# Pooled attention feeding two expert layers: pooled keys that carry the softmax scale, first scores in two halves, first values summed on TensorE

## The chip, the cores and the metric

The kernel runs as one program on one core of a Trainium2 chip. The metric is the device time of one execution in microseconds (us). A core has five engines that run side by side and meet at semaphores: TensorE (PE; its weight loads are listed as PEld), VectorE (DVE), ScalarE (ACT), GpSimd (POOL) and SyncE (SP), which issues nearly all of the transfers (DMA) between memory and the core. Each engine works through its own instructions strictly in the order in which the program lists them.

## The reference

Attention with pooled keys and values, then a layer of four gated experts, then a normalised gated layer. Only the first stage is touched:

```python
k_p = k.reshape(B, H, Sp, pool, D).mean(axis=3)      # B=4, H=8, S=576, D=64, pool=8, Sp=72
v_p = v.reshape(B, H, Sp, pool, D).mean(axis=3)
scores = scale * np.matmul(q, k_p.transpose(0, 1, 3, 2))   # scale = 1/sqrt(D)
scores = scores - np.max(scores, axis=-1, keepdims=True)
attn = np.exp(scores)
attn = attn / (np.sum(attn, axis=-1, keepdims=True) + 1e-09)
attn_out = np.matmul(attn, v_p)
# x = attn_out as 2304 tokens x 512
# then  out = sum_e p_e * relu(x @ w1[e]) @ w2[e],  E=4, F=1024
# then  (silu(xn @ w_gate) * (xn @ w_val)) @ w_out  with xn the rms-normalised out
```

## The kernel before

**Tiles.** The 2304 tokens are 18 tiles of 128. The expert layers run in three passes of six tiles. Tiles 0 to 5 are attended before and between the first expert products, tiles 6 to 17 beside them. A batch has 576 tokens, so tiles 0 to 3 use keys and values of batch 0 alone, tile 4 uses batches 0 and 1, and tile 5 batch 1.

**One tile of attention**, as steps with their names in the order table (i is the tile): `sc` is the scores (8 TensorE passes: four products of the queries of a pair of heads with the pooled keys `kpb`, each float32 product being two passes); `mx` is the row maximum and its multiplication by -SCALE (L1087, L1088, VectorE); `ex` is eight exponentials, one per head, with the scale and the maximum as operands and the row sum as a second output (L1094, ScalarE); `nm` normalises (L1106 to L1108, VectorE); `tr` is eight transposes (L1120, TensorE); `ca` and `cd` copy their two halves out of PSUM (ScalarE, VectorE); `av` is the product with the pooled values `vpb` (L1154, TensorE); `rw` copies it out (L1171, ScalarE); `ha`, `hd`, `l0`, `l1` cut it into a rounded part and a rest for the expert products.

**Pooling.** `Lk0a`, `Lk0b` load the keys of batch 0 (two pairs of heads each), `k0a`, `k0b` add the eight tokens of a pool (L1009, VectorE) and put the sums into `kpb` (L1016, ScalarE). `Lv0a` to `Lv0d` load the values of batch 0, two heads each. `v0a`, `v0b`, `v0c` add them on TensorE, by eight accumulating products with an identity matrix (L1042), and `vc` copies the sums out (L1049); `v0d` adds on GpSimd (L991, L1045). The values of batch 1 (`v1a` to `v1d`) are all added on GpSimd, its keys on VectorE with a copy into `kpb` by GpSimd (L1014). `Lv0d` and `Lv1c` use one buffer, `vr`: the second load waits until the first has been read.

**Order.** The text `ORDER` (L55 to L63) lists the steps up to the fourth expert block, and every engine gets its instructions in this order. `heatN` are N products of the identity with itself on TensorE, which nothing reads. `p000`, `p001` and so on are the first expert products (`by_half`, L558 to L560), which need tiles 0 to 2; `sc4`, the scores of tile 4, needs the pooled keys of batch 1. `ws0` prepares the first weights on GpSimd (L321 to L325), `wh0` rounds them on VectorE (L307), `t00`, `t10` on ScalarE (L331).

**Transfers.** SP issues in the order of the table and stops at the first one that may not go. Each transfer reports on one of eight semaphores in turn, so it waits, beside its buffer, for the landing of the one eight before it. The queries of tiles 0 and 1 go through ScalarE's queue.

Of the kernel before, what the change touches and what calls it, by code (L numbers as in the profile page):

```python
# [11 lines left out]
F32 = mybir.dt.float32  # L12
# [14 lines left out]
P = 128  # L27
NPAIR = H // 2
# [5 lines left out]
TT = NST // NPASS  # L34
# [17 lines left out]


ORDER = """
Lq0 heat24 Lk0a Lq1 k0a ow0 Lk0b k0b Lv0a or0 sc0 Lw0 Lv0b ws0 v0a xo mx0 ex0 Lv0d sc1 t00 v0d Lq2 wh0 Lv0c  # L55
mx1 ex1 v0b nm0 sc2 Lq3 mx2 ex2 nm1 tr0 cd0 nm2 Lx1 v0c ca0 tr1 ow2 Lv1c cd1 Lv1a vc av0 ca1 rw0 tr2 wl0 hd0
ha0 Lq4 av1 ca2 cd2 av2 l10 rw1 swap Lk1a sc3 Lk1b Lq5 hd1 ha1 l00 rw2 Lv1b v1b l11 ha2 Lx0 xh01 hd2 free0 l01
t10 l02 ow1 Lw1 l12 p000 heat12 mx3 k1a p001 xl01 ex3 r000 or1 s000 xh00 nm3 tr3 v1a wh1 k1b ca3 Ld cd3 av3
# [9 lines left out]
def tile_kernel(ctx: ExitStack, tc, qp, kp, vp, dp, w1r, w2r, w64, rg, out):  # L68
    nc = tc.nc
# [53 lines left out]
    xo = [{}, {}]  # L123
# [865 lines left out]
    def halve(cut):  # L989
        for w in (4, 2):  # L990
            nc.gpsimd.tensor_tensor(cut(0, w), cut(0, w), cut(w, 2 * w), op=ALU.add)  # L991

    def spare(tag):
        return late["sb"].tile([P, 4 * N], F32, name="stg", tag=tag, bufs=4 if tag == "hA" else 3)

    def pool_k(b, j, stage=None, eng=None):

        if stage is None:
            stage = at["sb"].tile([P, 2 * S], F32, name="kr", tag="kr")
        else:  # L1000
            stage = spare(stage)
        stage = stage[:, :2 * S].rearrange("p (j s k) -> p j s k", j=2, k=POOL)
        for i in range(2):
            nc.sync.dma_start(stage[:, i], kp[b, j + i].rearrange("p (s k) -> p s k", k=POOL))
        yield
        if eng is nc.vector:
            for i in range(2):
                c = at["sb"].tile([P, SP], F32, name="kc", tag="kc", bufs=2)
                nc.vector.tensor_reduce(c, stage[:, i], axis=AX.X, op=ALU.add)  # L1009
                for hh in range(2):  # L1010
                    sl = slice(64 * hh, 64 * hh + 64)
                    o = kpb[b % 2][sl, j + i, hh, :]
# [12 lines left out]
    def pool_v(b, h, stage=None, eng=None, queue=nc.sync):
# [35 lines left out]
    def att_a(i):  # L1061
        att_sc(i)
        att_ex(i)

    SCALE = 1.0 / (POOL * math.sqrt(D))

    def att_sc(i):
        q = q_t.pop(i)
        if at["few"]:
            sc = at["ps"].tile([P, 2, 512], F32, name="sc", tag="at")  # L1070
        else:
            sc = at["ps"].tile([P, 2, 512], F32, name="sc", tag="sc", bufs=2)
# [7 lines left out]
        es_t[i] = sc[:, :, 0:4 * SP].rearrange("p a (h s) -> p a h s", h=4)  # L1080

    def att_mx(i):
        v = es_t[i]
        m = at["sb"].tile([P, H], F32, name="m", tag="m", bufs=2)
        sm = at["sb"].tile([P, H], F32, name="sm", tag="sm", bufs=2)
        es = at["sb"].tile([P, H, SP], F32, name="es", tag="es", bufs=2)
# [12 lines left out]
    def att_a(i):
        att_sc(i)  # L1100
        att_mx(i)
        att_ex(i)
# [100 lines left out]
    def run(queue, k=1, one=False):  # L1203
# [165 lines left out]
    for si, ((moe, p), ids) in enumerate(stages):  # L1369
# [3 lines left out]
        for i in ids[2 * (si == 0):]:  # L1373
            k, _, e, r = quads[i]
# [132 lines left out]
```

## Time and profile before

| | |
|---|---|
| time, median of 3 runs | 1265.5 us (1264.29 to 1267.74) |
| profiled execution, span from first to last instruction | 1264.4 us |
| TensorE busy | 1242.1 us, 98% of the span |
| VectorE, ScalarE, GpSimd busy | 833.4, 529.3, 264.6 us |
| first expert product | at 27.27 us |

The span is that of one execution under the profiler; the runs were timed without it. The span ends with the last instruction, and no separate time of the profiled execution is listed, so the median stands beside it: it is 1.1 us more. A busy engine need not be the one that the others wait for, and a share of the span is a mean over stages that differ: the first 40 us are attention and loading, the rest is dominated by products of 384 and 512 columns.

### The profile page before, as it was taken

The page shows a single profiled execution, that of the slowest core. Times are in us where ns is not written, and L with a number is a line of the kernel's source. Part 1 is how long each engine was busy: PE and PEld are TensorE (multiplying, and loading weights), DVE is VectorE, ACT ScalarE, POOL GpSimd, SP SyncE. Part 2 cuts the span into 40 slices and gives each one's busy share as a digit, 9 for nine tenths or more (in the row PEclk, how much of TensorE's full clock was granted, in tenths as well). Part 3 has the DMA queues.
Part 4 walks back from the last instruction along what each step waited for, and adds up shares of the span by engine and source line. Part 5 has one row for each costly group of instructions (what it writes and reads, how often), then busy time and mean ns, then how long its engine had stood idle before and what let it go on. Part 6 is the DMA issues. An engine that isn't in the chain of part 4 may idle for free.

```text
span 1264.4 us, 18367 instructions
## 1 busy us (share of the span) xinstructions
PE 1242.1 (98%) x6876; PEld 1149.0 (91%) x6876; DVE 833.4 (66%) x1335; ACT 529.3 (42%) x1211; POOL 264.6 (21%) x252
## 2 busy tenths in 40 slices
PE   8999999999999999999999999999999999999998
PEld 8889888988898888888889998888999999999998
DVE  6866656656557766644877776475567765786575
ACT  6564544444453333323443343255454434434331
POOL 3434433420112222200333332131220000000000
PEclk9999999999999999999999999999999999999999
DMA  8488687778787777665889988667777777867671
GB/s 262 164 314 300 241 288 252 278 288 303 262 304 266 264 285 268 230 236 198 311 300 346 317 322 304 248 229 278 301 289 272 256 292 263 307 249 298 225 268 51
DMA packets 118937, 339.15 MB, mean 268 GB/s; under 512 B 10304, under 2 KB 48192, under 8 KB 99648
## 3 DMA queue, kind: packets, MB, share of 16 engines
q1 hardware_dynamic: 118560, 337.46, 73.7%
q8 instruction: 54, 0.88, 0.3%
q10 hardware_dynamic: 288, 0.52, 0.1%
q14 instruction: 35, 0.29, 0.1%
HBM read 233.61 MB, written 104.33 MB: 267 GB/s over the span
## 4 chain that ended last, share of the span: by engine, by line
PE 83%; DVE 8%; DMA 4%; ACT 3%; issue 1%; POOL 0%; SPq 0%; ACTq 0%; DVEq 0%; POOLq 0%
PE py L876 9%; PE py L875 9%; PE py L874 9%; PE qX L523 8%; PE qX L525 8%; PE qX L524 8%; PE qY L523 4%; PE qY L525 4%; PE qY L524 4%; PE qZ L523 2%; PE qZ L525 2%; PE qZ L524 2%; DMA wt<-wt_d 1%; PE gy L821 1%; DMA wc_d<-cx 1%; PE gy L823 1%
## 5 line engine op out<-in xcount | busy, mean ns | idle before, releaser
L892 DVE SCALAR_TENSOR_TENSOR y<-py,dps,y 128x512 f32<-128x512 f32 x126 | 94.4, 750 | 180.9 <-PE py L876 180.8
L438 POOL TENSOR_TENSOR cx<-cx 128x512 f32<-128x512 f32 x36 | 50.2, 1394 | 381.7 <-ACT hB L578 84.9
L523 PE MATMUL qX<-xos,wt 128*128 128x384 f32 x328 | 113.6, 346 | 6.5 <-ACT s L531 4.5
L876 PE MATMUL py<-w,hB 128*128 128x512 f32 x288 | 113.6, 395 | 0.0
L875 PE MATMUL py<-w,hB 128*128 128x512 f32 x288 | 113.4, 394 | 0.0
L876 PE MATMUL py<-w,hA 128*128 128x512 f32 x288 | 113.4, 394 | 0.0
L875 PE MATMUL py<-w,hA 128*128 128x512 f32 x288 | 113.4, 394 | 0.0
L874 PE MATMUL py<-w,hA 128*128 128x512 f32 x288 | 112.4, 390 | 0.0
L874 PE MATMUL py<-w,hB 128*128 128x512 f32 x288 | 112.1, 389 | 0.0
L525 PE MATMUL qX<-xos,wt 128*128 128x384 f32 x328 | 111.2, 339 | 0.0
L524 PE MATMUL qX<-xos,wt 128*128 128x384 f32 x328 | 110.8, 338 | 0.0
L578 ACT ACTIVATE hB<-u 128x768 fp32r<-128x768 f32 x46 | 39.1, 849 | 141.3 <-DVE u L535 138.7
L528 ACT ACTIVATE qZ<-qX 128x384 f32<-128x384 f32 x81 | 38.9, 480 | 118.2 <-PE qX L525 83.1
L533 DVE TENSOR_TENSOR u<-qY,s 128x384 f32<-128x384 f32 x82 | 45.5, 554 | 64.6 <-PE qY L525 34.1
L531 ACT ACTIVATE s<-qX 128x384 f32<-128x384 f32 x83 | 40.7, 490 | 108.5 <-PE qX L525 108.5
L263 POOL TENSOR_TENSOR tw<-rw 128x512 f32<-128x512 f32 x25 | 36.8, 1474 | 222.4 <-DVE wt L281 168.9
L523 PEld LDWEIGHTS qX<-xos,wt 128*128 128x128 f32 x328 | 61.9, 189 | 14.3 <-ACT s L531 6.2
L876 PEld LDWEIGHTS py<-w,hB 128*128 128x128 f32 x288 | 54.0, 188 | 11.6 <-DVE hB L564 0.2
L524 PEld LDWEIGHTS qX<-xos,wt 128*128 128x128 f32 x328 | 61.9, 189 | 2.7
L876 PEld LDWEIGHTS py<-w,hA 128*128 128x128 f32 x288 | 54.0, 188 | 11.4
L874 PEld LDWEIGHTS py<-w,hA 128*128 128x128 f32 x288 | 54.2, 188 | 10.1 <-issue 0.2
L875 PEld LDWEIGHTS py<-w,hA 128*128 128x128 f32 x288 | 54.0, 188 | 10.2 <-DVE w L378 0.3
(224 smaller groups left out, 3514.4 us busy)
## 6 DMA issues: line engine op xcount, KB each, us to landing
wt<-wt_d SPq DMA_DIRECT2D x56, 1024.0 KB
w<-w_d SPq DMA_DIRECT2D x32, 1024.0 KB
wt_d<-wt SPq DMA_DIRECT2D x28, 1024.0 KB
wr<-wr_d SPq DMA_DIRECT2D x56, 512.0 KB
wr_d<-wr SPq DMA_DIRECT2D x28, 768.0 KB
cr<-w SPq DMA_DIRECT2D x36, 512.0 KB
w<-ws_d SPq DMA_DIRECT2D x18, 1024.0 KB
w_d<-w SPq DMA_DIRECT2D x16, 1024.0 KB
```

The costliest lines, as they stand in the source:

```text
L438: nc.gpsimd.tensor_tensor(x, x, m.bitcast(F32), op=ALU.mult)
L523: nc.tensor.matmul(bank[b], wh, xh, start=first and k == 0, stop=False, **kw)
L524: nc.tensor.matmul(bank[b], wh, xl, start=False, stop=False, **kw)
L525: nc.tensor.matmul(bank[b], wl, xh, start=False, stop=k == 1, **kw)
L528: nc.scalar.activation(v, bank[b], AF.Copy)
L531: nc.scalar.activation(s[n], bank[b], AF.Copy)
L533: nc.vector.tensor_tensor(u[:, 0], bank["Y"], s[2], op=ALU.add)
L578: nc.scalar.activation(h[:, 0], u, AF.Relu)
L874: nc.tensor.matmul(ps, lhs[0], w[:, 0, c], start=j == 0, stop=False)
L875: nc.tensor.matmul(ps, lhs[0], w[:, 1, c], start=False, stop=False)
L876: nc.tensor.matmul(ps, lhs[1], w[:, 0, c], start=False, stop=j == len(units) - 1)
L892: nc.vector.scalar_tensor_tensor(y_t[t], ps, gate, y_t[t], op0=ALU.mult, op1=ALU.add)
```

## The change

- The pooled keys hold minus SCALE times the sum, so that the row extreme of the raw scores is a minimum, which is the bias of the exponential as it stands; the multiplication of the maximum (L1088) is gone from every tile, and the exponential has scale -1. For batch 0 ScalarE's copy into `kpb` multiplies. For batch 1 GpSimd's copy becomes a multiplication. For batches 2 and 3 GpSimd's last addition goes over all 128 rows and two multiplications follow it.
- The keys of batch 0 are loaded and summed in four steps (`Lk00` to `Lk03`, `k00` to `k03`), pairs 0 and 2 through SP's queue and pairs 1 and 3 through ScalarE's. All queries go through SP's.
- Scores, minimum and exponentials of tile 0 are cut into two halves of four heads (`sc0l`, `mx0l`, `ex0l`, `sc0h`, `mx0h`, `ex0h`).
- `v0d` adds on TensorE, and `vc` copies all eight heads. `cc0`, a copy on VectorE, replaces `ca0` on ScalarE.
- The order table up to `p000` is written anew.

```diff
 ORDER = """
-Lq0 heat24 Lk0a Lq1 k0a ow0 Lk0b k0b Lv0a or0 sc0 Lw0 Lv0b ws0 v0a xo mx0 ex0 Lv0d sc1 t00 v0d Lq2 wh0 Lv0c
...
+Lk00 Lk01 heat18 Lq0 Lk03 Lk02 Lq1 ow0 or0 Lw0 Lq2 k00 k01 sc0l k02 k03 mx0l ex0l heat4 sc0h Lv0a mx0h ex0h xo
...
-                    if b:
-                        nc.gpsimd.tensor_copy(o, c[sl])
-                    else:
-                        nc.scalar.activation(o, c[sl], AF.Copy)
+                    nc.gpsimd.tensor_scalar(o, c[sl], -SCALE, None, op0=ALU.mult)
         else:
             halve(lambda a, b: stage[..., a:b])
+            nc.gpsimd.tensor_tensor(stage[..., 0], stage[..., 0], stage[..., 1], op=ALU.add)
             for hh in range(2):
                 sl = slice(64 * hh, 64 * hh + 64)
-                o = kpb[b % 2][sl, j:j + 2, hh, :]
-                nc.gpsimd.tensor_tensor(o, stage[sl, ..., 0], stage[sl, ..., 1], op=ALU.add)
+                nc.gpsimd.tensor_scalar(kpb[b % 2][sl, j:j + 2, hh, :], stage[sl, ..., 0], -SCALE, None, op0=ALU.mult)
...
+    def first_k(j, queue):
+        if j // 2 not in k_raw:
+            k_raw[j // 2] = spare("hA")[:, :2 * S].rearrange("p (j s k) -> p j s k", j=2, k=POOL)
+        queue.dma_start(k_raw[j // 2][:, j % 2], kp[0, j].rearrange("p (s k) -> p s k", k=POOL))
+
+    def first_k_sum(j):
+        c = at["sb"].tile([P, SP], F32, name="kc", tag="kc", bufs=2)
+        nc.vector.tensor_reduce(c, k_raw[j // 2][:, j % 2], axis=AX.X, op=ALU.add)
+        for hh in range(2):
+            sl = slice(64 * hh, 64 * hh + 64)
+            nc.scalar.activation(kpb[0][sl, j, hh, :], c[sl], AF.Copy, scale=-SCALE)
...
-        for j in range(NPAIR):
+        for j in pairs:
...
-        nc.vector.tensor_reduce(m.rearrange("p (a h) -> p a h", a=2), v, axis=AX.X, op=ALU.max)
-        nc.vector.tensor_scalar(m, m, -SCALE, None, op0=ALU.mult)
...
+        nc.vector.tensor_reduce(
+            m.rearrange("p (a h) -> p a h", a=2)[:, half], v[:, half], axis=AX.X, op=ALU.min
+        )
...
-        for h in range(H):
+        for h in heads:
             nc.scalar.activation(
-                es[:, h], v[:, h // 4, h % 4], AF.Exp, bias=m[:, h:h + 1], scale=SCALE, accum_out=sm[:, h:h + 1]
+                es[:, h], v[:, h // 4, h % 4], AF.Exp, bias=m[:, h:h + 1], scale=-1.0, accum_out=sm[:, h:h + 1]
             )
...
-    def att_cd(i):
+    def att_cd(i, a=1):
         aT, tr = aT_t[i]
-        nc.vector.tensor_copy(aT[:, 4:], tr[1])
-        tr[1] = None
+        nc.vector.tensor_copy(aT[:, 4 * a:4 * a + 4], tr[a])
+        tr[a] = None
...
-        (0, "hA", nc.tensor), (2, "hB", nc.tensor), (4, "hB", nc.tensor), (6, None, None)
+        (0, "hA", nc.tensor), (2, "hB", nc.tensor), (4, "hB", nc.tensor), (6, None, nc.tensor)
...
-        "swap": swap, "xo": first_xo, "gates": gates, "vc": lambda: v_copy(6),
+        "swap": swap, "xo": first_xo, "gates": gates, "vc": lambda: v_copy(8),
...
-        step(f"Lq{i}", load_q, i, nc.scalar if i < 2 else nc.sync)
+        step(f"Lq{i}", load_q, i)
+    for j in range(NPAIR):
+        step(f"Lk0{j}", first_k, j, nc.scalar if j % 2 else nc.sync)
+        step(f"k0{j}", first_k_sum, j)
+    for a, c in enumerate("lh"):
+        step("sc0" + c, att_sc, 0, range(2 * a, 2 * a + 2))
+        step("mx0" + c, att_mx, 0, slice(a, a + 1))
+        step("ex0" + c, att_ex, 0, range(4 * a, 4 * a + 4))
+    for i in range(TT):
+        step(f"cc{i}", att_cd, i, 0)
```

In the orders that follow, `sc<-kpb,y` are scores, `vs` the sums of values of batch 0 (two heads in eight products), `tr` transposes, `av` the products with the values. TensorE before, from the first instruction to the scores of tile 3:

```order
L1059 MATMUL heat<-ident 128x128 x24
L1076 MATMUL sc<-kpb_88,y 128x144 x4
L1042 MATMUL vs<-stg,ident 72x128 x8
L1076 MATMUL sc<-kpb_88,y 128x144 x4
L1042 MATMUL vs<-stg,ident 72x128 x8
L1076 MATMUL sc<-kpb_88,y 128x144 x4
L1120 MATMUL tr<-ident,es 72x128 x8
L1042 MATMUL vs<-stg,ident 72x128 x8
L1120 MATMUL tr<-ident,es 72x128 x8
L1154 MATMUL av<-aT,vpb_90 64x128 x8
L1120 MATMUL tr<-ident,es 72x128 x8
L1154 MATMUL av<-aT,vpb_90 64x128 x16
```

TensorE of the changed kernel in the same place, after its 18 first heat products, the first two score products of tile 0 and four heat products:

```order
L1095 MATMUL sc<-kpb_88,y 128x144 x2
L1070 MATMUL heat<-ident 128x128 x4
L1095 MATMUL sc<-kpb_88,y 128x144 x4
L1070 MATMUL heat<-ident 128x128 x2
L1053 MATMUL vs<-stg,ident 72x128 x8
L1095 MATMUL sc<-kpb_88,y 128x144 x4
L1053 MATMUL vs<-stg,ident 72x128 x8
L1142 MATMUL tr<-ident,es 72x128 x8
L1053 MATMUL vs<-stg,ident 72x128 x8
L1142 MATMUL tr<-ident,es 72x128 x8
L1053 MATMUL vs<-vr,ident 72x128 x8
L1176 MATMUL av<-aT,vpb_90 64x128 x16
```

There are 28 heat products in place of 24, ten of them behind the first scores; a fourth group of value sums, `vs<-vr`, stands behind the transposes of tile 1, and the products of tiles 0 and 1 with the values now stand behind it.

The start of TensorE's order in the changed kernel once more, with the semaphores that an instruction waits for (`DVE_49` and `Activation_49` count VectorE's and ScalarE's instructions, the `DMAHW` ones transfers):

```order
L1070 MATMUL heat<-ident 128x128 x17
L1095 MATMUL sc<-kpb_88,y 128x144 [waits DMAHW1_49,Activation_49,Pool_49]
L1095 MATMUL sc<-kpb_88,y 128x144 [waits Activation_49]
L1070 MATMUL heat<-ident 128x128 x4
L1095 MATMUL sc<-kpb_88,y 128x144 [waits DVE_49,Activation_49]
L1095 MATMUL sc<-kpb_88,y 128x144
L1070 MATMUL heat<-ident 128x128 x4
```

The third score product of tile 0 has a wait on VectorE, at the count of `mx0l`, and one on ScalarE, at the count of the fourth exponential of `ex0l`; before, the four products had waits on ScalarE for the pooled keys alone.

SP's queue before, from the load of `v0d` into `vr` (first row) to the next load into `vr`, that of `v1c`, and what follows it:

```order
L1034 DMA vr<-vp 72x1024 [waits DMAHW1_49]
L986 DMA y<-qp 128x512 [waits DMAHW2_49]
L1034 DMA stg<-vp 72x1024 [waits DMAHW3_49]
L986 DMA y<-qp 128x512 [waits DMAHW4_49]
L352 DMA stg<-w2r 128x1024 [waits DMAHW5_49]
L1034 DMA vr<-vp 72x1024 [waits DMAHW6_49,DMAHW1_49,Pool_49]
L1034 DMA stg<-vp 72x1024 [waits DMAHW7_49]
L986 DMA y<-qp 128x512 [waits DMAHW0_49]
```

The same place of SP's queue in the changed kernel:

```order
L1045 DMA vr<-vp 72x1024 [waits DMAHW3_49]
L986 DMA y<-qp 128x512 [waits DMAHW4_49]
L352 DMA stg<-w2r 128x1024 [waits DMAHW5_49,DVE_49]
L1045 DMA vr<-vp 72x1024 [waits DMAHW6_49,DMAHW3_49,PE_49]
L1045 DMA stg<-vp 72x1024 [waits DMAHW7_49]
L986 DMA y<-qp 128x512 [waits DMAHW0_49]
```

The load of `v1c` waited for GpSimd's sum of `v0d` and now waits for TensorE's; behind it, in both, stand the loads of `v1a`, of tile 4's queries, of the keys of batch 1, of tile 5's queries and of `v1b`.

## Rows read from the trace of the kernel before

**Rows 1.** The page, part 1: busy time of TensorE.

```profile
PE 1242.1 (98%) x6876; PEld 1149.0 (91%) x6876; DVE 833.4 (66%) x1335; ACT 529.3 (42%) x1211; POOL 264.6 (21%) x252
```

**Rows 2.** Windows: stretch, its length, busy time of each engine, clock, DMA.

```profile
9.24:27.27 18.03, 15.67 (x153) 13.96 (x152) 14.95 (x31) 13.52 (x62) 5.77 (x6) 1.00 0.88 267
27.27:38.70 11.43, 10.46 (x90) 9.49 (x89) 8.35 (x15) 7.01 (x25) 8.95 (x15) 1.00 0.32 106
```

**Rows 3.** Timeline of TensorE: start, duration, line, tile; idle time before in brackets.

```profile
1.39 7.85 PE L1059 MATMUL heat<-ident 128*128 128x128 f32 x48 [1.39 <-POOL ident masks.py:199]
...
10.06 1.91 PE L1042 MATMUL vs<-stg,ident 72*72 72x128 f32 x16
11.81 1.15 PE L1076 MATMUL sc<-kpb,y 128*128 128x144 f32 x8
...
21.54 1.09 PE L1154 MATMUL av<-aT,vpb 72*64 72x128 f32 x16
22.56 1.07 PE L1120 MATMUL tr<-ident,es 128*72 128x128 f32 x8
23.56 1.97 PE L1154 MATMUL av<-aT,vpb 72*64 72x128 f32 x32
26.28 1.25 PE L1076 MATMUL sc<-kpb,y 128*128 128x144 f32 x8 [0.76 <-ACT stg L1171]
27.27 0.43 PE L558 MATMUL qX<-xoa,wr 128*128 128x384 f32 x1
...
29.45 2.84 PE L1059 MATMUL heat<-ident 128*128 128x128 f32 x24
```

**Rows 4.** Timeline of TensorE at the scores of tile 4.

```profile
38.04 1.04 PE L1076 MATMUL sc<-kpb,y 128*64 128x144 f32 x6 [0.60 <-POOL kpb L1014]
```

**Rows 5.** Timeline of GpSimd up to 38.6 us.

```profile
16.19 0.85 POOL L1045 TENSOR_TENSOR vpb<-vr 72x128 f32<-72x128 f32 x1
28.96 2.41 POOL L991 TENSOR_TENSOR stg<-stg 72x512 f32<-72x512 f32 x2 [11.93 <-DMA stg<-vp]
31.45 0.45 POOL L1045 TENSOR_TENSOR vpb<-stg 72x128 f32<-72x128 f32 x1
31.85 1.56 POOL L1014 COPY kpb<-kc 64x72 f32<-64x72 f32 x4
33.49 2.08 POOL L991 TENSOR_TENSOR stg<-stg 72x512 f32<-72x512 f32 x2
35.64 1.87 POOL L1045 TENSOR_TENSOR vpb<-stg 72x128 f32<-72x128 f32 x1
37.46 1.11 POOL L1014 COPY kpb<-kc 64x72 f32<-64x72 f32 x4
```

**Rows 6.** Timeline of SP's issues: the loads of v1c and v1b.

```profile
17.06 0.32 SPq L1034 DMA_DIRECT2D vr<-vp  x1
...
20.72 0.35 SPq L1034 DMA_DIRECT2D stg<-vp  x1
```

**Rows 7.** Timeline of VectorE and ScalarE.

```profile
11.05 1.18 DVE L1088 TENSOR_SCALAR m<-m 128x8 f32<-128x8 f32 x1
...
12.33 0.32 ACT L1094 ACTIVATE es<-sc,m 128x72 f32<-128x72 f32 x1 [2.98 <-DVE m L1088]
...
13.53 0.33 ACT L1094 ACTIVATE es<-sc,m 128x72 f32<-128x72 f32 x1
...
23.67 0.69 DVE L1135 COPY aT<-tr 72x512 f32<-72x512 f32 x1
...
25.65 0.58 ACT L1171 ACTIVATE stg<-av 128x512 f32<-128x512 f32 x1
```

**Rows 8.** Windows of TensorE alone: length, busy, clock, DMA.

```profile
84.60:86.80 2.20, 0.14 (x1) 1.00 0.85 137
...
88.00:91.50 3.50, 3.50 (x13) 0.51 1.02 433
91.50:95.00 3.50, 3.50 (x19) 1.00 1.01 387
```

More of the change, by code (lines that the diff above doesn't have):

```diff
@@ L54 @@
 ORDER = """
-Lq0 heat24 Lk0a Lq1 k0a ow0 Lk0b k0b Lv0a or0 sc0 Lw0 Lv0b ws0 v0a xo mx0 ex0 Lv0d sc1 t00 v0d Lq2 wh0 Lv0c
-mx1 ex1 v0b nm0 sc2 Lq3 mx2 ex2 nm1 tr0 cd0 nm2 Lx1 v0c ca0 tr1 ow2 Lv1c cd1 Lv1a vc av0 ca1 rw0 tr2 wl0 hd0
-ha0 Lq4 av1 ca2 cd2 av2 l10 rw1 swap Lk1a sc3 Lk1b Lq5 hd1 ha1 l00 rw2 Lv1b v1b l11 ha2 Lx0 xh01 hd2 free0 l01
-t10 l02 ow1 Lw1 l12 p000 heat12 mx3 k1a p001 xl01 ex3 r000 or1 s000 xh00 nm3 tr3 v1a wh1 k1b ca3 Ld cd3 av3
+Lk00 Lk01 heat18 Lq0 Lk03 Lk02 Lq1 ow0 or0 Lw0 Lq2 k00 k01 sc0l k02 k03 mx0l ex0l heat4 sc0h Lv0a mx0h ex0h xo
+heat4 sc1 Lv0b wh0 mx1 ex1 heat2 v0a Lv0c nm0 Lv0d sc2 v0b ws0 mx2 tr0 ex2 cc0 cd0 Lq3 v0c nm1 wl0 tr1 v0d vc cd1
+av0 ca1 nm2 rw0 av1 tr2 ha0 hd0 rw1 Lx1 ca2 cd2 l00 av2 l10 ha1 hd1 l01 l11 Lv1c Lv1a Lq4 ow2 rw2 swap Lk1a sc3
+Lk1b Lq5 Lv1b v1b ha2 Lx0 xh01 hd2 free0 t00 t10 l02 ow1 Lw1 l12 p000 heat12 mx3 k1a p001 xl01 ex3 r000 or1 s000 xh00 nm3 tr3 v1a wh1 k1b ca3 Ld cd3 av3
 rw3 sc4 xh10 wl1 p100 Lv1d r001 Lx2 v1c pr0 mx4 s001 p101 ex4 gates hd3 sc5 or2 nm4 r101 r100 mx5 tr4 cd4 xl00
@@ L1012, in pool_k @@
                     o = kpb[b % 2][sl, j + i, hh, :]
-                    if b:
-                        nc.gpsimd.tensor_copy(o, c[sl])
-                    else:
-                        nc.scalar.activation(o, c[sl], AF.Copy)
+                    nc.gpsimd.tensor_scalar(o, c[sl], -SCALE, None, op0=ALU.mult)
         else:
             halve(lambda a, b: stage[..., a:b])
+            nc.gpsimd.tensor_tensor(stage[..., 0], stage[..., 0], stage[..., 1], op=ALU.add)
             for hh in range(2):
                 sl = slice(64 * hh, 64 * hh + 64)
-                o = kpb[b % 2][sl, j:j + 2, hh, :]
-                nc.gpsimd.tensor_tensor(o, stage[sl, ..., 0], stage[sl, ..., 1], op=ALU.add)
+                nc.gpsimd.tensor_scalar(kpb[b % 2][sl, j:j + 2, hh, :], stage[sl, ..., 0], -SCALE, None, op0=ALU.mult)
         yield
+    k_raw = {}
+    def first_k(j, queue):
[8 more added lines that the diff above has]
+            nc.scalar.activation(kpb[0][sl, j, hh, :], c[sl], AF.Copy, scale=-SCALE)
     def pool_v(b, h, stage=None, eng=None, queue=nc.sync):
@@ L1065, in tile_kernel, with att_sc @@
     SCALE = 1.0 / (POOL * math.sqrt(D))
-    def att_sc(i):
-        q = q_t.pop(i)
-        if at["few"]:
+    sc_t = {}
+    def att_sc(i, pairs=range(NPAIR)):
+        q = q_t[i]
+        if i in sc_t:
+            sc = sc_t.pop(i)
+        elif at["few"]:
             sc = at["ps"].tile([P, 2, 512], F32, name="sc", tag="at")
@@ L1072, in att_sc @@
             sc = at["ps"].tile([P, 2, 512], F32, name="sc", tag="sc", bufs=2)
-        for j in range(NPAIR):
+        if NPAIR - 1 in pairs:
+            q_t.pop(i)
+        else:
+            sc_t[i] = sc
+        for j in pairs:
             o = (j % 2) * 2 * SP
@@ L1079, in att_sc, with att_mx, att_ex @@
                 )
[L1080 to L1086, printed above, removed]
-        nc.vector.tensor_reduce(m.rearrange("p (a h) -> p a h", a=2), v, axis=AX.X, op=ALU.max)
-        nc.vector.tensor_scalar(m, m, -SCALE, None, op0=ALU.mult)
-        es_t[i] = es, sm, m, v
-    def att_ex(i):
-        es, sm, m, v = es_t[i]
-        for h in range(H):
+        es_t[i] = es_t.get(i, ()) or (sc[:, :, 0:4 * SP].rearrange("p a (h s) -> p a h s", h=4),)
+    def att_mx(i, half=slice(0, 2)):
+        if len(es_t[i]) == 1:
+            m = at["sb"].tile([P, H], F32, name="m", tag="m", bufs=2)
+            sm = at["sb"].tile([P, H], F32, name="sm", tag="sm", bufs=2)
+            es = at["sb"].tile([P, H, SP], F32, name="es", tag="es", bufs=2)
+            es_t[i] = es, sm, m, es_t[i][0]
+        es, sm, m, v = es_t[i]
+        nc.vector.tensor_reduce(
+            m.rearrange("p (a h) -> p a h", a=2)[:, half], v[:, half], axis=AX.X, op=ALU.min
+        )
+    def att_ex(i, heads=range(H)):
+        es, sm, m, v = es_t[i]
+        for h in heads:
             nc.scalar.activation(
-                es[:, h], v[:, h // 4, h % 4], AF.Exp, bias=m[:, h:h + 1], scale=SCALE, accum_out=sm[:, h:h + 1]
+                es[:, h], v[:, h // 4, h % 4], AF.Exp, bias=m[:, h:h + 1], scale=-1.0, accum_out=sm[:, h:h + 1]
             )
-        es_t[i] = es, sm
+        if H - 1 in heads:
+            es_t[i] = es, sm
     def att_a(i):
@@ L1215, in tile_kernel @@
     pair = [quads[0], quads[1]]
-    k0 = [pool_k(0, j, "hA", nc.vector) for j in (0, 2)]
     v0 = [pool_v(0, h, t, e) for h, t, e in (
-        (0, "hA", nc.tensor), (2, "hB", nc.tensor), (4, "hB", nc.tensor), (6, None, None)
+        (0, "hA", nc.tensor), (2, "hB", nc.tensor), (4, "hB", nc.tensor), (6, None, nc.tensor)
     )]
@@ L1258, in tile_kernel @@
     for i in range(TT + 2):
-        step(f"Lq{i}", load_q, i, nc.scalar if i < 2 else nc.sync)
+        step(f"Lq{i}", load_q, i)
[8 more added lines that the diff above has]
+        step(f"cc{i}", att_cd, i, 0)
     for j, c in enumerate("ab"):
-        step("Lk0" + c, next, k0[j])
-        step("k0" + c, next, k0[j])
         step("Lk1" + c, next, k1[j])
```

## The prediction

> **What bounds the kernel now.** I read the busy times first. TensorE works 1242.1 of 1264.4 us [rows 1], so a change that leaves its products alone can only win or lose in the 22 us in which it does not run, or by adding products. Next, the windows of the start, since the change is there: between the end of the first heat products (1.39 + 7.85 = 9.24) and the first expert product (27.27) TensorE is busy 15.67 of 18.03 us [rows 2, 3]. That leaves 2.36 us of idle time. So the prologue is not a chain of exponentials with TensorE at leisure; TensorE itself is close to full there. In the next stretch, up to the scores of tile 4, it is busy 10.46 of 11.43 us [rows 2].
>
> Then I asked which wait ends last there. The scores of tile 4 wait 0.60 us for GpSimd's copies of the pooled keys of batch 1 [rows 4]. GpSimd had idled 11.93 us until a transfer of values, that of `v1b`, landed at 28.96, and from there it works without a pause to 38.57 [rows 5]. That transfer was issued at 20.72, the last of a run of loads which began at 17.06 with `v1c` [rows 6], and `v1c` began when GpSimd had finished the sum of `v0d` (16.19 + 0.85 = 17.04) [rows 5]. So there are two chains to the scores of tile 4: TensorE's own order, and `v0d`, `v1c`, `v1b`, GpSimd, which today ends 0.60 us after the first. Behind these scores TensorE's order holds everything else, so a delay there stays.
>
> **TensorE's order, step by step.** Prices are the distances between starts in [rows 3]: a heat product is two passes of 2.84/24 = 0.118 us; a group of value sums 11.81 - 10.06 = 1.75; the scores of a tile 27.27 - 26.28 = 0.99; eight transposes 23.56 - 22.56 = 1.00; one tile times the values 22.56 - 21.54 = 1.02.
>
> Eighteen heat products in place of 24 end 12 passes sooner, at 9.24 - 12 x 0.118 = 7.8. Then come half scores 0.5, heat4 0.94, half scores 0.5, heat4 0.94, scores 0.99, heat2 0.47, values 1.75, scores 0.99, values 1.75, transposes 1.00, values 1.75, transposes 1.00 and the new values 1.75: 14.3 us in all. Without any wait `v0d` is summed at 22.15. The keys need not be earlier for that; the load through two queues is hidden behind the heat products, and I count it at nothing. If it failed to hide, at the worst it would be as late as today, when the scores began at about 9.2, and the loss would be under 1.4 us; that lies in the range.
>
> **The halves.** The trace of before shows no halves. The second half of the scores waits for the fourth exponential of the first half (the count in the order). So the halves follow one another instead of overlapping: half scores end at 8.3, the minimum over half the columns takes about 0.4, four exponentials 13.53 - 12.33 = 1.2 [rows 7] and the readout of the last sum some 0.15, which makes 10.1. Heat4 ends at 9.3, so TensorE waits about 0.85. Bounds: nothing, if ScalarE is that much sooner, and 1.3 if the keys are as late as the reductions allow. With 0.85, and 0.2 for the two copies and the normalisation that VectorE does between the transposes of tiles 0 and 1, `v0d` is summed at 23.2 (22.15 to 23.8).
>
> **The removed multiplication.** It cost 1.18 us at tile 0 [rows 7], on the path to the exponentials. They do start earlier, near 8.8 and not at 12.33. But with TensorE's order as above they are no longer what ends last; I count 0 of this gain at `p000`, and the time won turns into waits of ScalarE for TensorE. In tiles 6 to 17 the operation lies beside expert products; 12 of them at most some 0.2 us each, and covered, count 0 (0 to -1). The longer GpSimd work for batches 2 and 3 (three more instructions each of four times) lies beside products too: 0 (0 to +0.5).
>
> **The first expert product.** Behind 23.2: the copy of the sums (as the 512 columns at 25.65) 0.6, two tiles times the values 2.0, transposes 1.0, copy 0.69 [rows 7], the second half of tile 2 0.5, its copy 0.58, scores of tile 3 1.0: 29.6 in place of 27.27, 2.3 later. So TensorE gives back more than the earlier keys bring: it has 1.75 for `v0d` and 8 x 0.118 = 0.94 for four more heat products to carry, and 2.36 us of idle time could not swallow both and the new waits.
>
> **The load of v1c.** It now waits for TensorE's sum of `v0d`, 23.2 in place of 17.04: 6.1 later (5.1 to 6.7). Queued behind it on SP are `v1a`, the queries of tile 4, both key loads of batch 1, the queries of tile 5 and `v1b`; SP goes in order, so all of them are 6.1 later. The transfer queue had run dry at 17 and is dry at 23 too, so I take the distance from `v1c` to the landing of `v1b` as it is, 28.96 - 17.06 = 11.9. GpSimd starts at 35.1. From its start to the point where the scores of tile 4 go on it took 38.04 - 28.96 = 9.1. At the least, with the cheaper of each pair in [rows 5], it is 2.08 + 0.45 + 1.11 + 2.08 + 0.45 + half of 1.11, 6.7. The multiplications for copies are not in the trace; bounds are the copies at 1.11 and 1.56 for four, from either side. I take 8.2, nearer to the measured chain, because VectorE, which also waits in its order for these copies before it can sum the second keys, will disturb GpSimd less. The scores of tile 4 go on at 43.3 in place of 38.04: **5.3 us later** (41.8 to 44.2 at 35.1; with the bounds of 23.2, 2.7 to 6.7 later). TensorE would be there 1.7 later by its own order alone (2.3 less the 0.60 wait), so it idles about 3.5 us more before and within these scores.
>
> **Sum.** 1264.4 + 5.3 = 1269.7 us of span. The median of the runs, 1265.5, lies 1.1 above the span; I add this: 1270.8. I see nothing behind tile 4 that gives time back, since TensorE is dense there and the transfers follow its progress.
>
> **A rule weighed.** After an idle stretch of 2.06 of 2.20 us the granted clock was 0.51 from 88.0 to 91.5, the 1.2 GHz level, with 13 products in 3.5 us against 19 in the next 3.5 at 1.00 [rows 8]: a price of 3.5 x (1 - 13/19) = 1.1 us. The Trainium skill (TensorE: Matmul & The Clock Gate, "What's actually happening") says that the throttled clock is the resting state and that the activity of the array lifts it; these rows agree. The new idle time before tile 4 is of that length, broken by one tile times the values; by the rule the sum would be 1271.9, without it 1270.8. I leave it out of the sum and keep it as a rival.
>
> **Rivals.**
> 1. Clock falls at tile 4: 1270.8 + 1.1 = 1271.9. For it: the length of the idle time as at 84.6 to 86.8. Against: the products with the values lie in the middle of it.
> 2. Only TensorE's own delay counts: the run of loads is faster on an empty queue, or GpSimd needs 6.7 and less. With `v1b` before 33 the scores of tile 4 are 1.7 to 2.3 later: about 1267.5. Against it: the queue was as empty at 17.
> 3. TensorE has room: the sums of `v0d` fit into its idle time and end before 17.04. Then `v1c` goes sooner than today, at 15 say, and the scores of tile 4 come as much as 2 us sooner: 1263.5. It decides at the end of `vs<-vr` against 17.04. For it speaks ScalarE: 24 exponentials at 0.3 from 8.8 would be done at 16. Against it: 14.3 us of products stand before that point, and they cannot end before 22.
> 4. The halves overlap after all: 0.85 less on both chains, 1270; inside the forecast.
>
> **Chances.** Forecast 0.57 (its own range 1268.4 to 1272.3), the clock 0.14, only TensorE 0.15, room on TensorE 0.09, something else 0.05. About 0.3%, 3.8 us, is what can be told from no change. Slower needs 1269.3: of the forecast 0.50, the clock 0.14, 0.03 of the rest: 0.67. Within: 0.07 of the forecast, 0.15, 0.05 of the third rival and its like: 0.27. Faster 0.06. The range goes from 1264.5, which leaves out most of the third rival, to 1273.8: the high bound of 6.7, 1.1 for the clock and 0.5 for GpSimd's longer work.
>
> **What would show it.** In the profile after: `vs<-vr` ends near 23; the load of `v1c` is issued right behind it; GpSimd's first sum of batch 1 starts near 35 with a wait on a transfer of about 20 us; TensorE's wait for `kpb` at tile 4, and the one before its product with the values of tile 3, grow to 3 us or more; the first expert product stands near 29.6; the exponentials of tile 0 start near 9 with a pause between the halves. It is wrong if `v1c` is issued before 20, or if `v1b` lands within 10 us of it.

## The result, and the profile after

The changed kernel takes 1274.24 us (median of 4 runs, 1273.86 to 1275.56), against 1266.62 for the kernel before in the same comparison: a ratio of 1.0056, interval 1.0043 to 1.0069. It is slower, as forecast, and by more: 7.6 us where 5.3 were forecast, and 1274.24 lies just above the upper end of the range, 1273.8 (the kernel before took 1.1 more in this comparison than the 1265.5 that the forecast started from). The profiled execution spans 1272.1 us at a mean granted clock of 0.997; before it was 1264.4 at 0.999. So 7.7 us have to be found.

The page, part 1, of the kernel after, beside [rows 1]: TensorE's busy time grew by 2.8 us, the products at a lower clock included; that is less than the loss of 7.7.

```profile
PE 1244.9 (98%) x6900; PEld 1151.9 (91%) x6900; DVE 828.6 (65%) x1319; ACT 528.9 (42%) x1210; POOL 267.3 (21%) x253
```

Windows of the start of after, with the columns of [rows 2]: length, busy time of each engine, granted clock, DMA share, GB/s. The first stretch ends with the first expert product, the second shortly before the end of tile 4's scores.

```profile
8.20:30.43 22.23, 19.16 (x186) 17.73 (x185) 12.85 (x31) 13.24 (x62) 2.71 (x3) 1.00 0.59 168
30.43:46.99 16.56, 11.32 (x89) 9.84 (x88) 7.78 (x14) 7.63 (x26) 8.96 (x14) 0.90 0.44 147
```

In the second stretch TensorE stands idle for 5.24 of 16.56 us, where in [rows 2] it did for 0.97 of 11.43. The timeline of TensorE says where; it answers to [rows 3] and [rows 4].

```profile
7.71 0.66 PE L1095 MATMUL sc<-kpb,y 128*128 128x144 f32 x4
8.20 1.05 PE L1070 MATMUL heat<-ident 128*128 128x128 f32 x8
10.30 0.76 PE L1095 MATMUL sc<-kpb,y 128*128 128x144 f32 x4 [1.05 <-ACT es L1115]
...
21.75 1.91 PE L1053 MATMUL vs<-vr,ident 72*72 72x128 f32 x16
24.34 1.97 PE L1176 MATMUL av<-aT,vpb 72*64 72x128 f32 x32 [0.68 <-ACT vpb L1060]
...
30.43 0.43 PE L558 MATMUL qX<-xoa,wr 128*128 128x384 f32 x1
...
41.32 0.66 PE L1176 MATMUL av<-aT,vpb 72*64 72x128 f32 x8 [2.88 <-ACT aT L1152]
42.84 0.66 PE L1176 MATMUL av<-aT,vpb 72*64 72x128 f32 x8 [0.86 <-DVE aT L1157]
43.33 1.42 PE L1095 MATMUL sc<-kpb,y 128*64 128x144 f32 x10
46.08 0.75 PE L1095 MATMUL sc<-kpb,y 128*64 128x144 f32 x4 [1.33 <-POOL kpb L1013]
46.99 0.74 PE L1095 MATMUL sc<-kpb,y 128*64 128x144 f32 x2 [0.16 <-POOL kpb L1013]
```

The first expert product is 3.16 us later than in [rows 3], and the scores of tile 4 go on at 46.08 in place of 38.04: 8.04 later. SP's issues show why: the loads of `v1c` and `v1b`, [rows 6] before.

```profile
23.69 0.33 SPq L1045 DMA_DIRECT2D vr<-vp  x1
...
27.65 0.33 SPq L1045 DMA_DIRECT2D stg<-vp  x1
```

GpSimd's timeline from there on, [rows 5] before:

```profile
36.97 2.06 POOL L991 TENSOR_TENSOR stg<-stg 72x512 f32<-72x512 f32 x2 [25.28 <-DMA stg<-vp]
39.11 0.45 POOL L1056 TENSOR_TENSOR vpb<-stg 72x128 f32<-72x128 f32 x1
39.65 1.76 POOL L1013 TENSOR_SCALAR kpb<-kc 64x72 f32<-64x72 f32 x4
41.49 3.08 POOL L991 TENSOR_TENSOR stg<-stg 72x512 f32<-72x512 f32 x2
44.65 0.45 POOL L1056 TENSOR_TENSOR vpb<-stg 72x128 f32<-72x128 f32 x1
45.18 1.75 POOL L1013 TENSOR_SCALAR kpb<-kc 64x72 f32<-64x72 f32 x4
```

And the chain of waits of after up to 50 us (start, length, what held it) joins these into one:

```profile
21.91 1.76 PE vs L1053 x16
23.69 3.94 DMA vr<-vp
27.65 9.16 DMA stg<-vp
36.87 0.10 issue
36.97 1.28 POOL stg L991
```

It is to be read from the bottom: GpSimd starts on a landing, that of `v1b`. `v1b` is the eighth transfer behind `v1c` and so reports on the same semaphore; it was issued when `v1c` had landed (23.69 + 3.94 = 27.63), and `v1c` when TensorE had summed `v0d`.

The other wait on TensorE, 2.88 us ahead of the values of tile 3, has the same root. ScalarE in after:

```profile
38.17 0.63 ACT L380 ACTIVATE w<-rw 128x512 fp32r<-128x512 f32 x1 [3.75 <-DMA rw<-w2r]
39.64 0.84 ACT L305 ACTIVATE wr<-rw 128x768 fp32r<-128x768 f32 x1 [0.84 <-DMA rw<-w1r]
...
40.70 0.57 ACT L1152 ACTIVATE aT<-tr 72x512 f32<-72x512 f32 x1
```

The copy for which TensorE waits (line 1152) stands behind the conversions of two tiles of weights, and ScalarE waits for both of them to land. Their loads follow `v1b` on SP's queue: they were issued at 29.28 and 29.78, before's at 22.26 and 23.56.

Then the clock. Windows of TensorE alone in after: length, busy time, granted clock, DMA.

```profile
43.00:46.00 3.00, 1.75 (x18) 0.59 0.00 0
46.00:49.00 3.00, 2.76 (x10) 0.50 0.00 0
49.00:52.00 3.00, 3.00 (x15) 0.77 0.00 0
52.00:55.00 3.00, 3.00 (x24) 1.00 0.02 5
...
96.00:98.00 2.00, 1.89 (x14) 1.00 1.04 438
```

From 43.6, for 6.8 us, the granted clock is 0.50, the 1.2 GHz level. Before there was none of this at tile 4; but before fell for 3.4 us at 88.0 [rows 8], where after, at the same place in its order, stays at 1.00.

The account of the 7.7 us: the scores of tile 4 are 8.04 late, those of tile 5 9.89 (53.17 against 43.28), so the clock, with a wait of 0.16 for GpSimd in between, took 1.85. The values of tile 6 are 7.71 late (104.03 against 96.32), mostly because before's own fall at 88.0 lies in between and after has none. Behind that the delay stays between 6.2 and 7.7 us nearly everywhere, and the span ends 7.7 late.

The 2.2 us given back at tile 6 are luck of this execution: a fall at this place stands in before's profile and in nine of the ten experiments' (between 86 and 98 us), and only after's and run 2's are without it.

### The profile page after: what moved, and what is told of

Read it like the earlier page. It is cut to its first block, busy times and chain, and to the rows that moved or that the text cites. A ratio compares the mean times of both kernels' runs of the same rounds, so it can differ in the third digit from the quotient of the medians.

```text
span 1272.1 us, 18386 instructions
## 1 busy us (share of the span) xinstructions
PE 1244.9 (98%) x6900; PEld 1151.9 (91%) x6900; DVE 828.6 (65%) x1319; ACT 528.9 (42%) x1210; POOL 267.3 (21%) x253
## 4 chain that ended last, share of the span: by engine, by line
PE 84%; DVE 7%; DMA 5%; ACT 2%; issue 1%; POOL 1%; SPq 0%; POOLq 0%; ACTq 0%; DVEq 0%
PE py L876 9%; PE py L875 9%; PE py L874 9%; PE qX L523 8%; PE qX L525 8%; PE qX L524 8%; PE qY L523 4%; PE qY L525 4%; PE qY L524 4%; PE qZ L523 2%; PE qZ L525 2%; PE qZ L524 2%; DMA wt<-wt_d 1%; DMA wc_d<-cx 1%; PE gy L821 1%; PE gy L823 1%
```

## The experiments

Each is compared with the kernel before on its own chip; before's median was 1266.76 to 1266.87. Runs 7, 8 and 9 change the kernel before, the others the kernel after. The program's order is the table quoted ahead; a line of it is cut to the names that move, and `...` stands for what is left out. Medians are of all runs, but a profile shows one execution; its time stands beside it where it is far from the median.

**1. v0d back to GpSimd.**

```diff
-(6, None, nc.tensor)   # v0d
+(6, None, None)
...
-"vc": lambda: v_copy(8)
+"vc": lambda: v_copy(6)
```

> The changed kernel with the last values of batch 0 (v0d) added on GpSimd again. Theory (the load of v1c waits for TensorE's sum of v0d, and with it all loads of batch 1 up to v1b, then GpSimd, then the scores of tile 4): v1c is issued near 17.5 and not at 23.7, GpSimd starts batch 1 near 30 and not at 37, the scores of tile 4 go on near 39.5 and not at 46.1, no half clock behind them; span about 1265.7, 6.4 under the changed kernel's 1272.1. Rival (TensorE's own extra products are what costs): only the 1.75 of the sums and the 0.68 of the wait behind them go, span about 1269.7.

1269.18 us, ratio 1.0023 (1.0010 to 1.0036): 5.1 us less than after. `v1c` is issued at 18.41 (after 23.69), GpSimd starts batch 1 at 31.43 and the scores of tile 4 go on at 40.98, so the chain moves as one. All three are 0.9 to 1.5 us later than I had said, and the clock, which I expected to hold, fell all the same (6.8 us from 39.7). Tile 4 is still 2.9 later than before: `v1c` goes 1.35 later, because GpSimd's sum of `v0d` starts later here (15.79; before 14.04), from `v1c` to GpSimd's start it takes 1.1 more, and GpSimd's own work 0.5 more.

**2. v0d stays on TensorE, v1c's and v1a's loads go behind v1b's.**

```diff
-l01 l11 Lv1c Lv1a Lq4 ... Lq5 Lv1b v1b
+l01 l11 Lq4 ... Lq5 Lv1b Lv1a Lv1c v1b
```

> The changed kernel with one edit in the order table: the load of v1c stands behind those of tile 4's and 5's queries, the keys of batch 1, v1b and v1a; v0d stays on TensorE and every product stays where it is. Theory: the first expert product stays near 30.4, but v1b lands before TensorE is through with the first expert products, the waits of 2.9, 0.9 and 1.3 us before the scores of tile 4 and the half clock behind them go, the scores of tile 4 start near 39.7 (before: 36.5), span about 1266.5, 5.6 under the changed kernel. Rival (TensorE's extra products): nothing on TensorE moves, span 1272.

1269.13, ratio 1.0013 (0.9998 to 1.0028; the profiled execution took 1265.59). This takes nothing from TensorE's work and wins the same 5.1 us. TensorE at the scores of tile 4:

```profile
40.16 1.15 PE L1095 MATMUL sc<-kpb,y 128*64 128x144 f32 x14
41.57 0.46 PE L1095 MATMUL sc<-kpb,y 128*64 128x144 f32 x2 [0.26 <-POOL kpb L1013]
```

Its wait for GpSimd is 0.26 in place of 1.33 and 0.16, and the waits on the values of tile 3 (2.88 and 0.86) have shrunk to one of 0.25; the clock doesn't fall there. So the late load was most of the loss, and not the sums as such. The edit moves `v1a` too; what `v1c` alone would do was not run. What is left is about 2.4 by the medians. It fits TensorE's own delay (its first expert product stands at 30.78, the scores of tile 5 at 46.24, 3.0 later than before), but the profile can't show it at the end: this execution has no fall of the clock at all, before's fall at 88.0 among them, and its span is 1263.8, 0.6 less than before's.

**3. The filler products between the first scores left out.** They only keep TensorE active; nothing reads what they compute.

```diff
-ex0l heat4 sc0h ... xo heat4 sc1 ... ex1 heat2 v0a
+ex0l sc0h ... xo sc1 ... ex1 v0a
```

> The changed kernel without the ten heat products behind the first scores (heat4, heat4, heat2); the 18 at the start stay. Theory: the first heat4 lies in the wait for the exponentials of the first half and gives nothing, the other two give 1.3 us on TensorE; the sum of v0d and the load of v1c come 1.3 earlier (22.4), and so does all behind them, span about 1270.8. Rival (the heat products fill idle time only, the exponentials decide): the load of v1c stays at 23.7, span 1272. Second rival (they hold the clock up): a half clock before 30 us, span above 1272.

1272.16, ratio 1.0050 (1.0030 to 1.0069), no clear difference from after. The profiled execution, which took 1277.44, shows the sign of my second rival; its windows, TensorE alone:

```profile
7.00:12.50 5.50, 2.54 (x21) 1.00 0.99 272
12.50:19.50 7.00, 6.57 (x31) 0.51 0.69 170
```

With TensorE busy 2.54 of 5.50 us the clock fell, and `v1c` went out at 26.96. In this execution the 10 products (2.4 us by the forecast's price) would have been worth their time; whether the clock fell there in the other five runs is not known. Taking them away isn't a repair.

**4. Tile 0 in one piece.**

```diff
-k00 k01 sc0l k02 k03 mx0l ex0l heat4 sc0h Lv0a mx0h ex0h xo
+k00 k01 k02 k03 heat4 sc0 Lv0a mx0 ex0 xo
```

> The changed kernel with the scores, the minimum and the exponentials of tile 0 in one piece, after the fourth keys; as many heat products, one heat4 in front of these scores. Theory (the halves wait for one another, so cutting costs TensorE its wait of 1.05 us): scores of tile 0 near 8.95 to 9.95, scores of tile 1 about 0.9 earlier than at 11.8, exponentials of tile 0 done near 13.2 (12.9 with halves), v1c issued near 22.8, span about 1271.2. Rival (the halves bring the exponentials forward and these decide): exponentials and all behind them later by 1 to 2 us, span above 1273.

1273.19, ratio 1.0052 (1.0031 to 1.0072). TensorE reaches the scores of tile 1 at 10.09 in place of 11.78 and those of tile 4 go on at 44.02 in place of 46.08: the halves cost 2 us there. In the median only 1.0 shows, inside the spread; the profiled execution took 1276.83 and spends 10.2 us at half clock from 38.7, so it can't say what reaches the end.

**5 and 6. The repairs together.** Run 5 is run 2 with tile 0 in one piece; run 6 also gives `v0d` back to GpSimd.

```diff
-k00 k01 sc0l k02 k03 mx0l ex0l heat4 sc0h Lv0a mx0h ex0h xo
+k00 k01 k02 k03 heat4 sc0 Lv0a mx0 ex0 xo
-l01 l11 Lv1c Lv1a Lq4 ... Lq5 Lv1b v1b
+l01 l11 Lq4 ... Lq5 Lv1b Lv1a Lv1c v1b
-(6, None, nc.tensor) ... v_copy(8)     # these two lines in run 6 only
+(6, None, None) ... v_copy(6)
```

> The changed kernel with v1c's load and sums put behind v1b's (as in the earlier run), and tile 0's scores and exponentials in one piece again; v0d stays on TensorE. My theory: the loss is v1c's late load, which GpSimd's chain to the scores of tile 4 hands on; what is left is TensorE's delay by v0d and the halves. Scores of tile 1 near 10.1 us, the first expert product near 29 (before 27.27), scores of tile 4 go on near 39 (before 38.04), no stretch at half clock there; span 1262.5 to 1264.5, median 1265 to 1267 against before's 1266.8. Rival, that the halves pay: slower than the run with v1c last alone, by 1 us or more.

> As the last one, and v0d's sums by GpSimd again: only the scale in the keys and the bias by a minimum, the two queues of the first keys and the later place of v1c are left of the change and its repair. My theory: TensorE waits for nothing new, so the first expert product comes at about 26.4 (before 27.27, since the two queues bring the first keys sooner), the scores of tile 4 go on 1 us before before's 38.04; span 1260.5 to 1262.5, median 1264.5 to 1265.5 against 1266.8. Rival, that TensorE's sums of v0d pay once v1c is out of their way: GpSimd's extra 4 us of sums hold up the values of chunk 0, and it is slower than the one with v0d on TensorE.

The profiled executions of the two took 1270.05 and 1266.52. Run 5: 1267.40, ratio 1.0003 (0.9992 to 1.0015), no different from before and just above the 1265 to 1267 that I expected. Run 6: 1264.71, ratio 0.9984 (0.9974 to 0.9994), faster than both kernels. `v0d` on TensorE costs 2.7 us even when `v1c` is out of its way; GpSimd has the room (it ends `v0d` at 18.7 and then waits for a transfer until 25.68). The time of run 6 was as I expected, but not its way there: its first expert product stands at 27.13, hardly ahead of before's 27.27, where I had said 26.4, and the last of tile 4's scores at 39.18, not ahead of before's at 38.62.

**7. Of the change only the scale in the keys and the minimum, in before's order.**

```diff
-nc.gpsimd.tensor_copy(o, c[sl])
+nc.gpsimd.tensor_scalar(o, c[sl], -SCALE, None, op0=ALU.mult)
...   # ScalarE's copy for batch 0 and GpSimd's work for batches 2 and 3, as in the change
-op=ALU.max) ... nc.vector.tensor_scalar(m, m, -SCALE, None, op0=ALU.mult) ... scale=SCALE
+op=ALU.min) ... scale=-1.0
```

> The kernel before with one part of the change alone: the scale multiplied into the pooled keys and the bias taken by a minimum, in before's order of work. My theory: the multiplication that goes was beside other work, and GpSimd's four multiplications for its copies cost 0.2 to 0.7 us a batch: span 1264.4 within 0.7, median no different from before's 1266.8 by more than 0.7. Rival, that the shorter score stage pays by itself: faster by 1.2 us or more.

Ratio 0.9999 (0.9986 to 1.0012; median 1267.79): no difference, as the forecast had it. But the profile shows two opposite effects and not one hidden operation: the first expert product comes 0.64 sooner (26.63), the scores of tile 4 go on 1.95 later (39.99) and the clock falls there. GpSimd starts batch 1 at 30.45 (before 28.96), and its four multiplications take 1.76 us where the copies took 1.56 and 1.11 [rows 5]. What the multiplication by itself is worth, this run does not separate. Nor is the operation as long as the 1.18 us of [rows 7] suggest: those ran beside an operation of two inputs on GpSimd (10.95 to 12.21), and at tile 2, at 17.43, where GpSimd stood idle, it took 0.17.

**8. Of the change only v0d on TensorE, in before's order, behind the scores of tile 1.**

```diff
-(6, None, None) ... v_copy(6)
+(6, None, nc.tensor) ... v_copy(8)
```

> The kernel before with one part of the change alone: v0d's sums by TensorE, put behind the scores of tile 1; VectorE and GpSimd have the rest as before, and v1c's load follows v0d's sums as in the changed kernel. There the scores stand early, so v1c is issued at about 15.6 us, 1.5 before before's 17.06. My theory, that the loss comes from v1c's lateness and not from TensorE's sums as such: GpSimd's chain is earlier than before, TensorE itself is about 2 us later at the first expert product (near 29.5), which is all that reaches tile 4's scores; span 1266.5, median 1268 to 1269.5. Rival, that only GpSimd's chain counts: not slower than before. If v1c is issued later than 18, the loss is the changed kernel's again (1270 or more).

1269.97, ratio 1.0030 (1.0017 to 1.0042; the profiled execution took 1271.73). Here `v1c` goes out at 16.04, a microsecond before [rows 6], and it is slower all the same, a little more than I expected. The timeline of TensorE:

```profile
14.04 1.97 PE L1042 MATMUL vs<-vr,ident 72*72 72x128 f32 x16 [1.02 <-DMA vr<-vp]
15.84 3.02 PE L1042 MATMUL vs<-stg,ident 72*72 72x128 f32 x16
18.66 2.12 PE L1076 MATMUL sc<-kpb,y 128*128 128x144 f32 x8
```

TensorE waits for `v0d` to land, sums it, and then the same sums take 3.02 in place of 1.91 and the scores 2.12 in place of 1.15: the granted clock was at 0.50 for 6.8 us from 16.5. So the first expert product stands at 31.92, where I had said 29.5. At tile 4 TensorE doesn't wait for GpSimd. So the rival that only GpSimd's chain counts falls. How much of the 3 us is the sums and how much the clock, this run does not separate.

**9. The kernel before with one move: v1c's and v1a's loads behind v1b's.**

```diff
-ow2 Lv1c cd1 Lv1a vc ... rw2 Lv1b v1b
+ow2 cd1 vc ... rw2 Lv1b Lv1a Lv1c v1b
```

> The kernel before with one move: the loads of v1c and v1a put behind v1b's. My theory: before, v1c's place already made GpSimd's chain end last, by 0.60 us at the scores of tile 4; with v1b loaded first that wait goes and TensorE's own order binds, so the scores of tile 4 go on 0.5 us earlier: span 1264 within 0.5, median 0 to 1 below before's 1266.8. So nearly all that the run with all three repairs won (2.1 us) would come from the first keys through two queues. Rival, that it is v1b's earlier load which won it: 1.5 us or more below.

1264.94, ratio 0.9987 (0.9976 to 0.9998): 1.9 below before, nearer the rival's size than mine, though the interval, 0.3 to 3.0, holds both. TensorE:

```profile
37.25 1.56 PE L1076 MATMUL sc<-kpb,y 128*64 128x144 f32 x16
...
43.01 1.14 PE L1076 MATMUL sc<-kpb,y 128*128 128x144 f32 x8
```

The 16 products run through without the 0.60 wait of [rows 4]. Only 0.27 of it is left at tile 5 in these two profiles (43.28 before). The rest I can show only as a tendency of the runs: the granted clock is 0.9983 on average over its 12 runs, 0.9973 over 78 runs of before. In those 78 runs a mean clock lower by 0.001 goes with about 1.0 us more (a straight line fitted to them), so this would be another 1.0, an estimate; why the clock is higher is not shown.

**10. Run 6 with v1c's load back ahead of v1b's.**

```diff
-l01 l11 Lq4 ... Lq5 Lv1b Lv1a Lv1c v1b     # - is run 6
+l01 l11 Lv1c Lv1a Lq4 ... Lq5 Lv1b v1b
```

> The run with all three repairs, with v1c's load back in the changed kernel's place (ahead of v1b's): of the change the scale, the minimum and the first keys' two queues stand. My theory: TensorE reaches the first expert product at 26.5 to 27.2, but v1c's load follows GpSimd's sum of v0d near 18.5, so GpSimd's chain to the scores of tile 4 ends 1 us or more after before's: median 1 to 2 above the run with all three repairs. Rival, that v1c's place is no matter once v0d is summed by GpSimd: no different from that run.

1269.03, ratio 1.0023 (1.0012 to 1.0034): 4.3 more than run 6, more than I had said. TensorE:

```profile
36.48 0.66 PE L1176 MATMUL av<-aT,vpb 72*64 72x128 f32 x8 [0.85 <-DVE aT L1157]
36.97 0.90 PE L1095 MATMUL sc<-kpb,y 128*64 128x144 f32 x10
39.73 0.49 PE L1095 MATMUL sc<-kpb,y 128*64 128x144 f32 x4 [1.86 <-POOL kpb L1013]
...
48.15 1.14 PE L1095 MATMUL sc<-kpb,y 128*128 128x144 f32 x8
```

and its windows:

```profile
38.00:40.00 2.00, 0.27 (x4) 1.00 0.00 0
40.00:46.80 6.80, 6.38 (x23) 0.50 0.00 0
46.80:50.00 3.20, 3.20 (x24) 0.99 0.00 0
```

The scores of tile 4 go on 1.69 after before's, those of tile 5 stand 4.87 after: the clock falls behind a wait of 1.86, and that, with a last wait of 0.42, costs 3.2 more. So with `v1c` ahead of `v1b`, no gain of the two queues for the first keys shows: the first expert product is 0.55 sooner than before's (26.72), and TensorE then waits longer at tile 4.

With tile 0 in one piece, four runs make a table of the two causes (medians in us, from three chips on which before's median differs by 0.1):

| | v0d on GpSimd | v0d on TensorE |
|---|---|---|
| v1c and v1a loaded ahead of v1b | 1269.03 (run 10) | 1273.19 (run 4) |
| v1c and v1a loaded behind v1b | 1264.71 (run 6) | 1267.40 (run 5) |

The place of these loads costs 4.3 to 5.8, TensorE's sum 2.7 to 4.2, and the halves 1.0 to 1.7 (after against run 4, run 2 against 5, their intervals overlapping).

## Why the prediction was right in direction and short in size

**TensorE's order: right, to 0.8.** `v0d` was forecast to be summed at 23.2 and `v1c` to go out then; it went at 23.69. TensorE waited 1.05 between the halves, 0.85 forecast. The first expert product was due at 29.6 and came at 30.43.

**The halves: right.** ScalarE's timeline in after:

```profile
8.93 0.32 ACT L1115 ACTIVATE es<-sc,m 128x72 f32<-128x72 f32 x1
...
10.03 0.21 ACT L1115 ACTIVATION_READ_ACCUMULATOR es<-sc,m 128x1 f32 x1
11.65 0.32 ACT L1115 ACTIVATE es<-sc,m 128x72 f32<-128x72 f32 x1 [1.41 <-DVE m L1108]
```

The exponentials start near 9 as forecast, 3.4 sooner than in [rows 7], then stand for 1.41: the second half's scores wait for the fourth exponential of the first. The 3.4 us didn't reach the end.

**The multiplication and the queues, counted at nothing: the sum held** (run 7 is no different from before, and run 9 reaches run 6's time without the two queues). That the multiplication was merely covered is not shown; run 7 has a gain and a loss that cancel.

**The load of v1c: the right mechanism, mis-sized.** "The scores of tile 4 go on at 43.3" failed by 2.8, in three terms. (a) `v1c` went 0.5 later than 23.2. (b) "I take the distance from `v1c` to the landing of `v1b` as it is, 11.9": it was 36.97 - 23.69 = 13.28. `v1b` had to wait for `v1c`'s landing (0.3 of the 1.4), and then took 9.32 from issue to GpSimd's start against 8.24. In the ten experiments that time lies between 7.5 and 9.4; what decides it I can't say, and one reading of it was no price to 0.1. (c) "I take 8.2" for GpSimd: it was 9.11. Two things were too small in it. The four multiplications took 1.76 and 1.75, above both bounds that were set for them (1.11 and 1.56). And I had argued that VectorE would disturb GpSimd less. It does not: the two adds at 41.49 take 3.08 in place of 2.06, beside this on VectorE:

```profile
42.71 0.94 DVE L311 TENSOR_TENSOR wr<-rw,wr 128x768 fp32r<-128x768 f32 x1
```

In before the same line ran from 35.92 to 36.86, beside the 1.87 in [rows 5]; that before's sum of 9.08 is so near to 9.11 is chance. The Trainium skill (GPSIMD Engine Reference, Specifications) says that GpSimd shares its interfaces to the core's on-chip memory (SBUF) with VectorE and contends, among others, with VectorE's instructions that read two inputs from it; both traces agree.

**The clock: the rival with 0.14 came in, on top of the forecast.** Its price was put at 1.1; it was 1.85 between tile 4 and tile 5 (the wait of 0.16 included), where the stretch at half clock lasted 6.8 us and not 3.5. The 1.1 was low in itself: the second window of [rows 8] holds longer products of 512 columns, so its 19 can't be set beside the 13. In before's timeline products of 384 columns start 0.32 us apart at half clock and 0.17 apart at full clock, which makes 3.4 x (1 - 0.17/0.32) = 1.6 us, an estimate. I doubted the rival because products with the values lie in the middle of the idle time. They don't prevent it. Read over the kernels, one execution each, with TensorE's waits from the product with the values of tile 3 to the last of tile 4's scores:

| kernel | waits, us | half clock there |
|---|---|---|
| before | 0.25 + 0.60 | none |
| runs 8, 9 | 0.24, 0.25 | none |
| runs 2, 5, 6 | 0.24 or 0.25, + 0.26 | none |
| run 10 | 0.25 + 0.85 + 1.86 + 0.42 | 6.8 from 40.0 |
| run 1 | 0.25 + 0.73 + 1.85 + 0.16 | 6.8 from 39.7 |
| run 7 | 0.57 + 0.89 + 1.86 + 0.16 | 6.8 from 39.4 |
| after | 2.88 + 0.86 + 1.33 + 0.16 | 6.8 from 43.6 |
| run 3 | 1.05 + 1.50 + 1.85 + 0.16 | 6.8 from 46.8 |
| run 4 | 2.67 + 0.25 + 0.69 + 0.17 | 10.2 from 38.7 |

The last waits of a row can lie behind the start of the fall: in after the clock had fallen before those of 1.33 and 0.16, in run 4 in the middle of that of 2.67.

The end of it, in spans: 2.7 more at tile 4, 1.9 for the clock, and 2.2 given back by tile 6, most of it because before's later fall did not come: 5.3 + 2.7 + 1.9 - 2.2 = 7.7. So "I see nothing behind tile 4 that gives time back" failed as well, and by luck it hid part of the other two.

**From the span to the time.** "I add this", 1.1, took the median of before for the time of its profiled execution. In the runs whose time and span are both listed, the time is 1.7 to 1.9 above the span of the same execution: after's profiled one took 1273.86 with 1272.1. Of the 3.4 between 1270.8 and 1274.24, then, 2.4 lie in the span, 0.7 in this step, and 0.4 between that execution and the median.

**The rivals.** Only TensorE's delay (1267.5) is near what is left when the load is taken out of the chain: run 5 with 1267.40, run 2 with 1269.13. Room on TensorE is refuted by after itself, where `vs<-vr` ends at 23.67 and not before 17.04, and by run 8, where `v1c` does go sooner than before and the time is still 3 us longer.

## What to carry to other kernels

When a step is moved to another engine, ask first which loads wait for its buffer, and what stands behind them on the queue that issues in order: here one late load held back the six steps of loads behind it, and the step's own work was the smaller part. A load whose data is needed late goes behind those needed early, whatever frees its buffer first: that one move made the kernel before 1.9 us faster (0.9987) and mended most of the changed one. Price a wait of TensorE of a few microseconds with the fall of the clock behind it. And look where the profiled execution lies among the runs before reading a loss of a few microseconds from it.

## What the runs showed of the hardware that was not expected

A fall of the clock can cost about as much as the waits that came before it: in run 10 3.2 us, a wait of 0.42 in it, behind waits of 0.25, 0.85 and 1.86. It does not follow from the length of the idle time alone. Ahead of the transposes of tile 6 TensorE stands for 2.11 us in before and 2.12 in after; in before the clock fell to 0.51 [rows 8], in after the window from 96.0 shows 1.00. What differs there I could not settle. The runs of one kernel differ along with their mean clock: those of run 1 go from 1264.67, with 0.999, to 1273.49 with 0.993, as far apart as the two kernels that were to be compared. So one profiled execution prices a term of the sum to about 2 us, an estimate from the 2.2 that a missing fall gave back here.
